# A state-space scan feeding a gated MLP: a new order of the first group's scan, weight conversion in wider pieces and in place, and state products side by side

## The chip, the cores and the metric

The kernel runs on one NeuronCore of a Trainium2 chip. Its engines work side by side, each through its own queue in order: TensorE (PE) multiplies matrices, VectorE (DVE) and ScalarE (ACT) work on elements, GpSimd (POOL) does small work, and SyncE (SP) issues most DMA transfers. An instruction whose input is not there holds everything behind it on its engine. The metric is device time in microseconds (us). Before the change the median of three runs is 408.18 us (408.10 to 408.22).

## The reference, cut to what matters

The first part is a Mamba-2 style scan over 4 batches of 8 heads, 768 positions, head size 32, state size 16. With `a` the decays, it is computed in chunks:

```
for c in chunks:
    cum = cumsum(log(clip(a, 1e-6, 1)))           # within the chunk
    L   = exp(cum_i - cum_j) for i >= j, else 0
    y   = ((C @ B.T) * L) @ x + (C @ state) * exp(cum)
    state = exp(sum(log a)) * state + sum_j B_j x_j * exp(cum_last - cum_j)
```

The second part takes the heads side by side as 3072 tokens of 256 features:

```
h = x @ w_in                       # 256 -> 2048
g = h * sigmoid(1.702 * h)
out = g @ w_out                    # 2048 -> 256
```

The weights arrive as 64-bit floats and the kernel makes 32-bit floats of them.

## The kernel before, in words

**Groups and pairs.** The 3072 tokens are six groups of 512 (`NG`). A group is two *pairs* (`p`) of 128-position chunks (`k` = 0, 1). Each group goes through a scan, then the MLP: sixteen `hidden` steps h0 to h15 (line 551: two matmuls each, then a SiLU into gT on ScalarE, line 554), and a projection. Group 0 projects with `project_all`: sixteen steps f0 to f15 of four matmuls (line 570) that add up in the two PSUM banks o0 and o1. Groups 1 to 5 interleave hidden steps with seven-product blocks (`product`, line 616).

**The scan of a pair.** The steps are functions. `pick_a` spreads decays by ScalarE; `fan` (line 310) broadcasts them by matmul; `decay_heads` (line 333) or, for later pairs, `decay` (line 292) runs VectorE scans that give L; `ends` (line 350) multiplies B by L's last column (Be). `turn_only` transposes B and C (line 418) and copies them out by ScalarE (BT, CT, C); `since_start` (line 439) scales C by the decay since the chunk's batch began, which `fan_rows` and `decay_fanned` or `decay_rows` make. `score` (line 454) computes C B^T in the PSUM area cb, `weigh` (line 465) multiplies L by it, `gain` (line 480) and `keep` (lines 494, 501) make the state, and `finish` adds up y: line 520 multiplies by states (`inter`), line 529 by L, and ScalarE copies y into yT (line 537). In `finish`, `inter` for k = 0 comes first, then the 16 products with L, then `inter` for k = 1 where the pair is not first of its batch.

**The weights.** They are cut in 16 pieces, eight of w_in and eight of w_out, of two 128-wide tiles each. `fetch` loads a piece (bits, 512 KB); eight bits buffers allow six loads ahead. `unpack` makes from the low words m (ScalarE, line 147), and from the high words e (VectorE, line 148: the exponent), z and p2 (ScalarE, lines 152, 153: a power of two) and u (VectorE, line 154: the mantissa). `join` then makes three VectorE passes: m += u - 7 (168), sign into p2 (170), and their product into w_in or w_out (176). The buffers e and z are single; u, m and p2 are double. `narrow(i)` unpacks piece i + 1 and then joins piece i.

**Order.** The program is written in the order in which every engine is to execute it, and `in_order` pins each engine to that order at the end. The scan of group 0 (pairs 0 and 1) is written out by hand ahead of the first hidden step. In hidden and project of group 0 the tables `in_hidden[0]` and `in_project[0]` say after or before which step a narrow, a scan step of pairs 2 and 3, or a load is placed. PSUM banks of the tag ff are four and go around between h, y, o, transposes and small products, so a new tile waits for the reader of the one whose bank it takes. The DMA queue of SP takes its transfers in order too.

Of the kernel before, what the change touches and what calls it, by code (L numbers as in the profile page):

```python
# [8 lines left out]
FP32 = mybir.dt.float32  # L9
U32 = mybir.dt.uint32  # L10
# [24 lines left out]
def kernel(  # L35
# [77 lines left out]

    PF = 2
    AHEAD = 6
    assert 2 * CG * PF == NF
    PIECES = [("in", f) for f in range(0, NF, PF)] + [("out", f) for f in range(0, NF, PF)]
    PN = PF * DM
    bits = {}

    def fetch(i, queue=nc.sync):
        if i >= len(PIECES):
            return
        name, f = PIECES[i]
        bits[i] = t = wide.tile([P, 2 * PN], U32, tag="bits", name=f"bits{i}", bufs=AHEAD + 2)
        if name == "in":
            src = moe_w_in[:, 2 * f * P:2 * (f + PF) * P].rearrange("(k p) e -> p k e", p=P)
            dst = t.rearrange("p (k e) -> p k e", k=NK)
        else:
            src = moe_w_out[f * P:(f + PF) * P, :].rearrange("(f p) e -> p f e", p=P)  # L130
            dst = t.rearrange("p (f e) -> p f e", f=PF)
        queue.dma_start(out=dst, in_=src)

    parts = {}

    def unpack(i):


        fetch(i + AHEAD)
        words = bits.pop(i).rearrange("p (e w) -> p e w", w=2)  # L140
        lo, hi = words[:, :, 0], words[:, :, 1]
        e = wide.tile([P, PN], U32, tag="e", name=f"e{i}", bufs=1)
        u = wide.tile([P, PN], U32, tag="u", name=f"u{i}")
        m = wide.tile([P, PN], FP32, tag="m", name=f"m{i}")
        z = wide.tile([P, PN], FP32, tag="z", name=f"z{i}", bufs=1)
        p2 = wide.tile([P, PN], U32, tag="p2", name=f"p2{i}")
        nc.scalar.activation(m, lo, AF.Copy, scale=2.0 ** -52)  # L147
        nc.vector.tensor_scalar(out=e, in0=hi, scalar1=0x7FF00000, scalar2=None,
                                op0=ALU.bitwise_and)


        nc.scalar.activation(z, e, AF.Relu, scale=-8.0, bias=edge[:, 0:1])  # L152
        nc.scalar.activation(p2, z, AF.Relu, scale=-1.0, bias=edge[:, 1:2])
        nc.vector.tensor_scalar(out=u, in0=hi, scalar1=0x000FFFFF, scalar2=0x41000000,
                                op0=ALU.bitwise_and, op1=ALU.bitwise_or)
        parts[i] = hi, u, m, p2

    def narrow(i):
        if i + 1 < len(PIECES):
            unpack(i + 1)  # L160
        join(i)

    def join(i):

        name, f = PIECES[i]
        hi, u, m, p2 = parts.pop(i)

        nc.vector.scalar_tensor_tensor(out=m, in0=u.bitcast(FP32), scalar=-7.0, in1=m,
                                       op0=ALU.add, op1=ALU.add)
        nc.vector.scalar_tensor_tensor(out=p2, in0=hi, scalar=0x80000000, in1=p2,  # L170
                                       op0=ALU.bitwise_and, op1=ALU.bitwise_or)
        if name == "in":
            dst, split = w_in[:, :, f * P:(f + PF) * P], NK
        else:
            dst, split = w_out[:, f:f + PF, :], PF
        nc.vector.tensor_tensor(  # L176
            out=dst, in0=m.rearrange("p (k e) -> p k e", k=split),
            in1=p2.bitcast(FP32).rearrange("p (k e) -> p k e", k=split), op=ALU.mult)


# [3 lines left out]
    def spread(n):  # L184
        if n - 4 in ra:
            ra[n] = ra[n - 4]
        else:
            ra[n] = wide.tile([P, NH * P], FP32, tag="bits", name=f"a{n}", bufs=AHEAD + 2)
        b, c = divmod(n, NC)
        nc.sync.dma_start(  # L190
            out=ra[n].rearrange("p (h i) -> p h i", h=NH),
            in_=scratch[b, c].unsqueeze(0).to_broadcast([P, NH, P]))
# [25 lines left out]
    rows_a(az, (nc.sync,))  # L218
    for i in range(2, AHEAD):
        fetch(i)  # L220
# [13 lines left out]
    for r in range(R):  # L234
# [3 lines left out]
                                channel_multiplier=1)  # L238


    whose = const.tile([32, NH, N], FP32, name="whose")
    nc.gpsimd.memset(whose, 1.0)
    nc.gpsimd.affine_select(out=whose, in_=whose, pattern=[[-1, NH], [0, N]],
                            compare_op=ALU.is_equal, fill=0.0, base=0, channel_multiplier=1)

    ident = const.tile([P, P], FP32, name="ident")
    make_identity(nc, ident)
    idents = const.tile([P, NH, P], FP32, name="idents")
    nc.gpsimd.tensor_copy(idents, ident.unsqueeze(1).to_broadcast([P, NH, P]))

# [11 lines left out]
    nc.gpsimd.tensor_tensor(out=own, in0=same[:, :HB], in1=same[:, HB:], op=ALU.add)  # L262

    starts = {}

    def clip(t, name):

        nc.vector.tensor_scalar(out=t, in0=t, scalar1=1e-6, scalar2=1.0,
                                op0=ALU.max, op1=ALU.min)
        starts[name] = const.tile([P, t.shape[1], 1], FP32, name=f"starts{name}")  # L270
        nc.vector.tensor_copy(starts[name], t[:, :, 0:1])
        nc.vector.memset(t[:, :, 0:1], 0.0)

    clip(az0, 0)


# [19 lines left out]

    fans, flat = {}, {}

    def pick_a(p):

        b, c = divmod(2 * p, NC)
        X = fans[p] = ssd.tile([P, 2, Q, P], FP32, tag="CT", name=f"X{p}")
        for q in range(Q):
            nc.scalar.activation(X[:, :, q], (az if c + 2 > CG else az0)[:, c:c + 2], AF.Copy,
                                 scale=pick[:, b, q:q + 1])

    def fan(p, r, ab):
# [5 lines left out]

    def fan_all(p):
        ab = area(f"ab{p}")
        for r in range(R):
            fan(p, r, ab[:, r])
        fans[p] = ab

# [7 lines left out]
    def decay_heads(p, r, ab):  # L327

        if r == 0:
# [6 lines left out]
            initial=0.0, op0=ALU.mult, op1=ALU.add)  # L336

    def decay_pair(p, engine=nc.vector):
        ab = fans.pop(p)
        for r in range(R):  # L340
            decay_heads(p, r, ab[:, r])
        ends(p, 0, engine)
        ends(p, 1, engine)

# [160 lines left out]

    def finish(p):
        g, half = divmod(p, PG)
# [16 lines left out]

        inter(0 if c else 1, True, False)
        for k in range(2):
            for h in range(NH):
                t, q = divmod(h, HB)
                nc.tensor.matmul(  # L529
                    out=y[t][D * q:D * q + D, k], lhsT=rx[p][:, k, h],  # L530
                    rhs=L[:, k, h // Q, h % Q],
                    start=False, stop=True, tile_position=(0, D * q), skip_group_check=True)
        if c:
            inter(1, False, True)
# [49 lines left out]
    def mix_w(n):  # L584

        t = wide.tile([P, 2, 4, P], FP32, tag="bits", name=f"mw{n}", bufs=AHEAD + 2)
        w = w_out[:, 4 * n:4 * n + 4].rearrange("p (j i) (c e) -> p j i c e", i=2, c=2)
# [73 lines left out]

    rows_zero()
    keep_busy(2)
    for p in range(PG):
        pick_a(p)
    for r in range(R):
        fan_one(0, r)
    for r in range(R):
        decay_heads(0, r, ab[0, r])
    ends(0, 0, nc.gpsimd)  # L670
    ends(0, 1, nc.gpsimd)
    fan_rows(0, CG)
    decay_fanned(0, CG)
    turn_only(0)
    score(0)
    unpack(0)
    fan_one(1, 0)
    fan_one(1, 1)
    weigh(0)
    decay_heads(1, 0, ab[1, 0])  # L680
    decay_heads(1, 1, ab[1, 1])
    gain(0)
    fan_one(1, 2)
    fan_one(1, 3)
    keep(0)
    since_start(0)
    decay_heads(1, 2, ab[1, 2])
    decay_heads(1, 3, ab[1, 3])
    fans.clear()
    turn_only(1)  # L690
    score(1)
    ends(1, 0, nc.gpsimd)
    ends(1, 1, nc.gpsimd)
    finish(0)
    since_start(1)
    gain(1)
    weigh(1, (0, 1))
    keep(1)
    finish(1)
    join(0)  # L700
    clip(az, 1)
    for b in range(NB):
        nc.sync.dma_start(out=scratch[b].rearrange("c h s -> h c s"),
                          in_=az[b * NH:(b + 1) * NH])
    unpack(1)
    narrow(1)

# [9 lines left out]
    in_project = [{} for _ in range(NG)]  # L717
    for i, k in zip(range(2, 10), (0, 1, 3, 5, 6, 8, 13, 14)):
        at(in_hidden[0], k, lambda i=i: narrow(i))
    at(in_hidden[0], 7, lambda: pick_a(PG))  # L720
    at(in_hidden[0], 8, lambda: fan_rows(CG, NC), lambda: decay_fanned(CG, NC))
    at(in_hidden[0], 9, lambda: fan_all(PG), lambda: decay_pair(PG))
    for k in range(2):
        at(in_hidden[0], 1 + 2 * k, lambda k=k: spread(CG + 2 + k))
        at(in_hidden[0], 15, lambda k=k: decay(CG + 2 + k))
    for i, k in zip(range(10, 16), (2, 3, 5, 7, 9, 11)):
        at(in_project[0], k, lambda i=i: narrow(i))
    scan_at(in_project[0], PG, (0, 1, 4, 6))
# [121 lines left out]
```

## Time and profile before

| What | us |
|---|---|
| Median of the runs | 408.18 |
| Time of the profiled execution | 408.12 |
| Its span | 406.4 |
| First h matmul | 33.99 |
| Hidden steps of group 0 end, first transpose of pair 2 | 65.1 |
| First h matmul of group 1 | 103.06 |
| TensorE busy | 387.3 |
| VectorE busy | 233.5 |
| ScalarE busy | 121.0 |

The profile is of one execution. A busy time is the time in which an instruction of that engine was running. A line of the order of time gives the start, the length, the engine, the line of the kernel, the operation, what it writes and reads, the count, and in brackets how long the engine stood idle before and which instruction's end released it. A matmul of 32-bit floats is two records. PEld is the loading of weights into the array. DMA shares are means over 16 DMA engines.

### The profile page before, as it was taken

How to read it: one execution, taken by the hardware profiler on the slowest of the kernel's cores; microseconds unless marked ns; L12 is line 12 of the kernel's file. 1: busy time of each engine (PE TensorE's matmuls, PEld its weight loads, DVE VectorE, ACT ScalarE, POOL GpSimd, SP SyncE). 2: the span in 40 equal slices, each digit the busy share in tenths (PEclk: the TensorE clock that was granted, in tenths of full speed). 3: DMA queues.
4: the chain of work that ended last, by engine and by line, in shares of the span. 5: the costliest groups of instructions: out<-in, count | busy, mean ns of one | idle time of the engine just before them, and what ended most of it. 6: DMA issues, size and time to landing. Idle time of an engine off the chain costs nothing.

```text
span 406.4 us, 5086 instructions
## 1 busy us (share of the span) xinstructions
PE 387.3 (95%) x2012; PEld 246.3 (61%) x2012; DVE 233.5 (57%) x380; ACT 121.0 (30%) x229; POOL 10.5 (3%) x32
## 2 busy tenths in 40 slices
PE   5787999899999999999999999999999999999984
PEld 1443446678556678566668566668566668466662
DVE  1888998994779877753574753563651311531312
ACT  3316967460332212231212231212322211312111
POOL 5000000010000001000000000000000000000000
PEclk9999999999999999999999999999999999999999
DMA  9988735930898200078000070000010000000001
GB/s 155 268 133 231 247 117 123 163 129 2 122 252 110 62 0 2 0 253 110 2 0 0 2 258 2 0 0 2 0 53 0 2 0 0 29 24 0 0 2 52
DMA packets 86126, 29.52 MB, mean 73 GB/s; under 512 B 75800, under 2 KB 79064, under 8 KB 86104
## 3 DMA queue, kind: packets, MB, share of 16 engines
q1 hardware_dynamic: 81848, 28.55, 29.9%
q10 hardware_dynamic: 4256, 0.66, 1.0%
q8 instruction: 16, 0.26, 0.3%
q14 instruction: 6, 0.05, 0.0%
HBM read 25.95 MB, written 3.24 MB: 72 GB/s over the span
## 4 chain that ended last, share of the span: by engine, by line
PE 81%; SPq 5%; DVE 4%; DMA 4%; ACT 3%; issue 2%; ACTq 0%; DVEq 0%
PE h L551 37%; PE acc L616 30%; SPq L111 5%; PE o L570 4%; PE y L529 3%; PE cb L454 2%; PE y L520 2%; DMA af<-in_a_dram 1%; DMA bits<-in_moe_w_in_dram 1%; ACT z L152 1%; DVE L L292 1%; PE oT L648 1%; PE tp L418 1%; DMA c<-in_C_dram 1%; ACT m L147 1%
## 5 line engine op out<-in xcount | busy, mean ns | idle before, releaser
L551 PE MATMUL h<-yT,w_in 128*128 128x512 f32 x384 | 173.1, 596 | 2.9 <-DVE w_in L176 2.4
L551 PEld LDWEIGHTS h<-yT,w_in 128*128 128x128 f32 x384 | 71.6, 190 | 80.5 <-issue 71.8
L554 ACT ACTIVATE gT<-h 128x512 f32<-128x512 f32 x96 | 56.9, 595 | 171.1 <-PE h L551 133.4
L600 DVE TENSOR_TENSOR mg<-gT 128x512 f32<-128x512 f32 x40 | 27.6, 689 | 95.6 <-ACT gT L554 92.4
L616 PE MATMUL acc<-mg,mw 128*128 128x256 f32 x240 | 58.3, 379 | 0.7 <-ACT u L629 0.7
L616 PEld LDWEIGHTS acc<-mg,mw 128*128 128x128 f32 x240 | 45.5, 190 | 7.3 <-ACT u L629 1.1
L616 PE MATMUL acc<-gT,w_out 128*128 128x256 f32 x160 | 41.7, 384 | 0.6 <-DVE u L640 0.6
L292 DVE TENSOR_TENSOR_SCAN L<-a,idents 128x1024 f32<-128x1024 f32 x18 | 41.1, 2283 | 0.0
L616 PEld LDWEIGHTS acc<-gT,w_out 128*128 128x128 f32 x160 | 29.5, 190 | 15.6 <-issue 11.5
L465 DVE TENSOR_TENSOR L<-L,cb 128x2048 f32<-128x2048 f32 (+1 forms) x13 | 27.5, 2122 | 9.3 <-PE cb L454 9.3
L570 PE MATMUL o<-w_out,gT 128*128 128x256 f32 x128 | 29.6, 384 | 0.8 <-DVE w_out L176 0.8
L570 PEld LDWEIGHTS o<-w_out,gT 128*128 128x128 f32 x128 | 23.7, 190 | 5.0 <-DVE w_out L176 1.2
L616 PE MATMUL acc<-gT,mw 128*128 128x256 f32 x80 | 23.6, 380 | 0.8 <-DVE c L640 0.8
L616 PE MATMUL acc<-mg,w_out 128*128 128x256 f32 x80 | 23.6, 380 | 0.8 <-DVE u L640 0.8
L454 PE MATMUL cb<-CT,BT 32*128 32x256 f32 x192 | 15.6, 445 | 2.4 <-ACT CT L425 2.4
L602 DVE TENSOR_TENSOR mg<-gT,mg 128x256 f32<-128x256 f32 x40 | 17.0, 425 | 1.4
L601 DVE TENSOR_TENSOR mg<-gT,mg 128x256 f32<-128x256 f32 x40 | 17.0, 425 | 1.4
L616 PEld LDWEIGHTS acc<-gT,mw 128*128 128x128 f32 x80 | 15.1, 190 | 3.3 <-DVE c L640 1.2
L616 PEld LDWEIGHTS acc<-mg,w_out 128*128 128x128 f32 x80 | 15.1, 190 | 3.2 <-DVE u L640 1.2
L640 DVE TENSOR_TENSOR u<-acc,u 128x256 f32<-128x256 f32 (+1 forms) x10 | 5.6, 559 | 19.8 <-ACT u L629 14.0
L537 ACT ACTIVATE yT<-y 128x256 f32<-128x256 f32 x24 | 8.0, 380 | 28.9 <-PE y L520 16.1
L333 DVE TENSOR_TENSOR_SCAN L<-ab,idents 128x512 f32<-128x512 f32 x12 | 13.8, 1205 | 4.5 <-PE ab L310 4.5
(82 smaller groups left out, 275.2 us busy)
## 6 DMA issues: line engine op xcount, KB each, us to landing
a<-scratch SPq DMA_DIRECT2D x18, 512.0 KB, 7.0
bits<-in_moe_w_in_dram SPq DMA_DIRECT2D x8, 512.0 KB, 5.9
bits<-in_moe_w_out_dram SPq DMA_DIRECT2D x8, 512.0 KB, 4.3
out_dram<-ob SPq DMA_DIRECT2D x12, 256.0 KB, 2.2
x<-in_x_dram SPq DMA_DIRECT2D x20, 128.0 KB, 3.5
b<-in_B_dram SPq DMA_DIRECT2D x24, 64.0 KB, 3.2
c<-in_C_dram SPq DMA_DIRECT2D x24, 64.0 KB, 4.9
af<-in_a_dram SPq DMA_DIRECT2D x3, 384.0 KB
```

The costliest lines, as they stand in the source:

```text
L111: queue.dma_start(out=dst[p][:, k], in_=src[b, :, sl, :].rearrange("h s d -> s h d"))
L292: nc.vector.tensor_tensor_scan(out=Ls[p][:, k].rearrange("p r q i -> p (r q i)"), data0=ra[n], data1=idents.rearrange("p h i -> p (h i)"), ...
L333: nc.vector.tensor_tensor_scan(out=flat[p][:, r], data0=ab, data1=idents.rearrange("p h i -> p (h i)")[:, :2 * Q * P], initial=0.0, op0=AL ...
L454: nc.tensor.matmul(out=cb[:, r, k], lhsT=BT[rows, k], rhs=CT[rows, k].rearrange("p q i -> p (q i)"), start=True, stop=True, tile_position= ...
L465: nc.vector.tensor_tensor(out=Lv[:, k], in0=Lv[:, k], in1=cb.rearrange("p r k e -> p k r e")[:, k], op=ALU.mult)
L551: nc.tensor.matmul(out=h, lhsT=w_in[:, k, f * P:(f + 1) * P], rhs=yT[g][:, k], start=(k == 0), stop=(k == NK - 1))
L554: nc.scalar.activation(gT[g, j][:, i], h, AF.Silu, scale=GELU_SCALE)
L570: nc.tensor.matmul(out=o[k // 2][:, k % 2], lhsT=gT[g, f // 2][:, f % 2, k * P:(k + 1) * P], rhs=w_out[:, f], start=(f == 0 and k % 2 == 0 ...
L600: nc.vector.tensor_tensor(out=t[:, 0:2], in0=B[:, :, 1], in1=B[:, 0], op=ALU.subtract)
L601: nc.vector.tensor_tensor(out=t[:, 2], in0=B[:, 1, 1], in1=t[:, 0], op=ALU.subtract)
L602: nc.vector.tensor_tensor(out=t[:, 3], in0=B[:, 1, 0], in1=t[:, 2], op=ALU.subtract)
L616: nc.tensor.matmul(out=acc[g][:, i], lhsT=lhsT, rhs=rhs, start=(j == 0 and i % 2 == 0), stop=(j == NF // 2 - 1), skip_group_check=True)
```

## The change

It has three parts.

1. **The first group's scan.** The hand-written order of pairs 0 and 1 changes on all engines: fans and scans are interleaved, the transposes of pair 0 come ahead of the since-start row and those of pair 1 directly after the weighting of pair 0, since_start of pair 1 comes before its weighting, and part of the conversion of pieces 0 and 1 is moved. There are three warming matmuls instead of two. `clip`, `pick_a` and the identity tiles are made earlier. The tile X takes a buffer of the output tile ob. Clipping the whole of `a` and storing it to the scratch tensor (`store_a`) moves from ahead of h0 to after h4.
2. **The weights.** There are ten pieces: four of two tiles (in 0 to 7), then six of four tiles. Bits buffers are four of twice the size, and also hold two spread rows of `a` or two sets of mixed weights. `fetch` is called at named places only. u is written over the low words, e, z and p2 share a tile, and m is a step of its own, `lower`. `narrow(i)` now joins piece i, then fetches, then lowers piece i + 2, then unpacks piece i + 1.
3. **State products of y.** In `finish` the `inter` of k = 1 stands directly after that of k = 0, except for pair 1.

Lines of the diff that matter, with parts left out:

```diff
-    PF = 2
-    AHEAD = 6
-    PIECES = [("in", f) for f in range(0, NF, PF)] + [("out", f) for f in range(0, NF, PF)]
+    PIECES = [("in", f, 2) for f in range(0, 8, 2)] + [("in", 8, 4), ("in", 12, 4)] \
+        + [("out", f, 4) for f in range(0, NF, 4)]
+    PN = 4 * DM
+    BUFS = 4
+    def words(name):
+        return wide.tile([P, 2 * PN], U32, tag="bits", name=name, bufs=BUFS)
...
+    def lower(i):
+        low[i] = wide.tile([P, PN], FP32, tag="m", name=f"m{i}")[:, :PIECES[i][2] * DM]
+        nc.scalar.activation(low[i], bits[i][0], AF.Copy, scale=2.0 ** -52)
     def unpack(i):
-        fetch(i + AHEAD)
...
-        nc.scalar.activation(m, lo, AF.Copy, scale=2.0 ** -52)
+        e = wide.tile([P, PN], U32, tag="p2", name=f"p2{i}")[:, :PIECES[i][2] * DM]
         nc.vector.tensor_scalar(out=e, in0=hi, scalar1=0x7FF00000, scalar2=None,
                                 op0=ALU.bitwise_and)
+        z = e.bitcast(FP32)
         nc.scalar.activation(z, e, AF.Relu, scale=-8.0, bias=edge[:, 0:1])
-        nc.scalar.activation(p2, z, AF.Relu, scale=-1.0, bias=edge[:, 1:2])
-        nc.vector.tensor_scalar(out=u, in0=hi, scalar1=0x000FFFFF, scalar2=0x41000000,
+        nc.scalar.activation(e, z, AF.Relu, scale=-1.0, bias=edge[:, 1:2])
+        power[i] = e
+        nc.vector.tensor_scalar(out=lo, in0=hi, scalar1=0x000FFFFF, scalar2=0x41000000,
                                 op0=ALU.bitwise_and, op1=ALU.bitwise_or)
-    def narrow(i):
-        if i + 1 < len(PIECES):
-            unpack(i + 1)
-        join(i)
+    NEXT = {4: (7,), 5: (8,), 7: (9,)}
+    def narrow(i):
+        join(i)
+        for n in NEXT.get(i, ()):
+            fetch(n)
+        if i + 2 < len(PIECES):
+            lower(i + 2)
+        if i + 1 < len(PIECES):
+            unpack(i + 1)
...
+        if c and not late:
+            inter(1, False, False)
         for k in range(2):
             for h in range(NH):
...
-        if c:
+        if c and late:
             inter(1, False, True)
...
-    rows_zero()
-    keep_busy(2)
-    for p in range(PG):
-        pick_a(p)
+    keep_busy(3)
     for r in range(R):
         fan_one(0, r)
-    for r in range(R):
         decay_heads(0, r, ab[0, r])
+    rows_zero()
+    lower(0)
+    turn_only(0)
+    fan_rows(0, CG)
+    decay_fanned(0, CG)
     ends(0, 0, nc.gpsimd)
     ends(0, 1, nc.gpsimd)
-    fan_rows(0, CG)
-    decay_fanned(0, CG)
-    turn_only(0)
+    unpack(0)
     score(0)
-    unpack(0)
-    fan_one(1, 0)
-    fan_one(1, 1)
     weigh(0)
-    decay_heads(1, 0, ab[1, 0])
-    decay_heads(1, 1, ab[1, 1])
+    turn_only(1)
+    for r in range(2):
+        fan_one(1, r)
+        decay_heads(1, r, ab[1, r])
     gain(0)
-    fan_one(1, 2)
-    fan_one(1, 3)
     keep(0)
     since_start(0)
-    decay_heads(1, 2, ab[1, 2])
-    decay_heads(1, 3, ab[1, 3])
-    fans.clear()
-    turn_only(1)
-    score(1)
+    for r in range(2, R):
+        fan_one(1, r)
+        decay_heads(1, r, ab[1, r])
     ends(1, 0, nc.gpsimd)
     ends(1, 1, nc.gpsimd)
-    finish(0)
     since_start(1)
-    gain(1)
+    lower(1)
+    score(1)
     weigh(1, (0, 1))
+    finish(0)
+    gain(1)
     keep(1)
-    finish(1)
-    join(0)
-    clip(az, 1)
-    for b in range(NB):
-        nc.sync.dma_start(out=scratch[b].rearrange("c h s -> h c s"),
-                          in_=az[b * NH:(b + 1) * NH])
-    unpack(1)
-    narrow(1)
+    finish(1, late=True)
+    narrow(0)
+    join(1)
+    fetch(6)
+    lower(3)
...
-    for i, k in zip(range(2, 10), (0, 1, 3, 5, 6, 8, 13, 14)):
+    at(in_hidden[0], 0, lambda: unpack(2))
+    for i, k in ((2, 1), (3, 3), (4, 6), (5, 9), (6, 13)):
         at(in_hidden[0], k, lambda i=i: narrow(i))
+    at(in_hidden[0], 4, store_a)
     at(in_hidden[0], 7, lambda: pick_a(PG))
     at(in_hidden[0], 8, lambda: fan_rows(CG, NC), lambda: decay_fanned(CG, NC))
-    at(in_hidden[0], 9, lambda: fan_all(PG), lambda: decay_pair(PG))
+    at(in_hidden[0], 10, lambda: fan_all(PG))
+    for i, k in ((7, 1), (8, 5), (9, 9)):
+        at(in_project[0], k, lambda i=i: narrow(i))
     for k in range(2):
-        at(in_hidden[0], 1 + 2 * k, lambda k=k: spread(CG + 2 + k))
-        at(in_hidden[0], 15, lambda k=k: decay(CG + 2 + k))
-    for i, k in zip(range(10, 16), (2, 3, 5, 7, 9, 11)):
-        at(in_project[0], k, lambda i=i: narrow(i))
+        at(in_hidden[0], 5 + k, lambda k=k: spread(CG + 2 + k))
+        at(in_project[0], 3 + 3 * k, lambda k=k: decay(CG + 2 + k))
```

## The prediction

> **What bounds the kernel now.** I read the page first (busy times, then the chain that ended last), then busy time by stage, then the order of time from 0 to 105 us.
>
> ```profile
> PE 387.3 (95%) x2012; PEld 246.3 (61%) x2012; DVE 233.5 (57%) x380; ACT 121.0 (30%) x229; POOL 10.5 (3%) x32
> ...
> PE 81%; SPq 5%; DVE 4%; DMA 4%; ACT 3%; issue 2%; ACTq 0%; DVEq 0%
> ```
>
> TensorE is 81% of the chain, so only what fills its idle time or takes work off it can help. By stage (columns: PE, PEld, DVE, ACT, POOL busy):
>
> ```profile
> 0.00:34.00 34.00, 24.77 (x173) 12.57 (x173) 21.68 (x36) 9.84 (x22) 7.21 (x23) 1.00 0.94 182
> 34.00:65.10 31.10, 29.64 (x76) 12.78 (x77) 28.72 (x56) 25.00 (x43) 0.74 (x1) 1.00 0.60 194
> 65.10:103.10 38.00, 36.50 (x271) 29.37 (x270) 31.09 (x48) 16.22 (x30) 1.24 (x3) 1.00 0.46 98
> ```
>
> The three rows are the start (before the first h matmul), hidden 0 and project 0. Hidden and project hold only 1.46 and 1.50 us of TensorE idleness, so the change can save little there and lose much. The start is a relay between engines. The order of time shows its last legs:
>
> ```profile
> 9.95 4.57 DVE L333 TENSOR_TENSOR_SCAN L<-ab,idents 128x512 f32<-128x512 f32 x4 [4.20 <-PE ab L310]
> 18.02 2.29 DVE L465 TENSOR_TENSOR L<-L,cb 128x2048 f32<-128x2048 f32 x1 [1.54 <-PE cb L454]
> 28.04 2.35 DVE L465 TENSOR_TENSOR L<-L,cb 128x1024 f32<-128x1024 f32 x2 [1.50 <-PE cb L454]
> 33.16 0.69 DVE L176 TENSOR_TENSOR w_in<-m,p 128x512 f32<-128x512 f32 x1
> 33.99 3.67 PE L551 MATMUL h<-yT,w_in 128*128 128x512 f32 x8 [1.43 <-DVE w_in L176]
> ```
>
> VectorE stands 1.5 us before each weighting, for the scores. Then the weight conversion, whose overlap decides the rest:
>
> ```profile
> 41.89 0.71 ACT L152 ACTIVATE z<-e,edge 128x512 f32<-128x512 uint32 x1
> 42.33 0.68 DVE L170 SCALAR_TENSOR_TENSOR p<-bits,p 128x512 uint32<-128x512 uint32 x1
> 42.62 0.72 ACT L153 ACTIVATE p<-z,edge 128x512 uint32<-128x512 f32 x1
> 43.04 0.69 DVE L176 TENSOR_TENSOR w_in<-m,p 128x512 f32<-128x512 f32 x1
> 43.65 0.42 DVE L148 TENSOR_SCALAR e<-bits 128x512 uint32<-128x512 uint32 x1
> ```
>
> ScalarE makes z and p2 of the next piece while VectorE joins this one. The period is 2.6 us (43.04 to 45.64) for two h tiles, which take TensorE 3.44 (4 records of 0.43 each). VectorE stays ahead.
>
> [...] 512-column records are 0.86 us apart at the start, 0.43 later. [...] 8 fan records take 1.07 us warm, not 3.4. [...] No 1024-wide conversion is in the trace. [...]
>
> **The change, part by part.** The changed program's order on each engine (no times in it) says who waits for whom; I put the measured durations on it. Joining piece i here means its L168, L170, L176.
>
> *Start.* VectorE's list is now nearly gapless: scans 9.95 to 14.55, carry and since 1.3, e and u 0.75, weighting 0 from 16.45 to 18.7 (before 20.3); the second pair's fan arrives 19.1; two scans 2.3; keep and since_start 0.95, to 22.4; two scans to 24.65; since_start 0.45; wait for Be on POOL to 25.3; weighting 1 to 27.65; keep 1.05; join(0) 2.0. w_in's first piece is ready at 30.75, before at 33.85: **gain 3.1**. The third warming matmul makes the first busy stretch 5.1 us long instead of 3.8. [...] If so fans and scores run at full clock and the piece is ready at 29.4: gain 4.5. I take the mean, 3.8.
>
> *Conversion.* narrow(i) now joins i first and unpacks i+1 after it. Nothing of i+1 can overlap the join: e waits (in VectorE's order) for the product, z for e, p2 for z, the next join for p2. And m of piece i+2 takes the buffer of piece i, so it waits for that product, at the head of ScalarE's queue, with z, p2 and the gT copies behind it. Period of a narrow piece: e 0.34 past the product + 0.09 + m's push and a gT 0.7 + z, p2 1.47 + sign 0.7 + product 0.7 = 4.0, against 3.44. Of a wide one: m 1.1, z 1.17, p2 1.17, sign 1.26, product 1.22 = 5.95, against 6.88 for four h. Cold start, product ends: join(0) 30.75, (1) 34.3, (2) 38.4, (3) 42.3, (4) 48.3. h2 waits 0.1, h4 0.6, h6 0.6; h8 waits for the first wide piece with only h6 and h7 to cover it: 5.95 - 3.44 = **2.5 us stall**. So h0 starts at 30.9, h2 34.5, h4 38.5, h6 42.5, h8 48.4. Before, hidden lost 1.46 in all. Width itself saves: a wide piece costs VectorE 4.7 us (0.6 + 0.6 + 1.13 + 1.13 + 1.22) against 5.2 for two narrow ones, but VectorE would now wait for ScalarE, so the saving goes into that wait.
>
> Next: rows and starts (0.9, after h8) hold VectorE to 51.3, since 0.8, join(5) 52.1 to 55.7, mask and u 1.2: scans of pair 2 start 56.9. They are 4.57 + Be 0.58 + join(6) 3.6: first w_out at 65.6. Then e of piece 7, and on ScalarE m, z, p2 (1.0 + 1.17 + 1.05), and only then gT of h14, at 69.5. The second bank of o waits for that gT (its bank). From scans to there: 12.7 us; TensorE has 5 h, a transpose and half of f0, 9.9, and reaches the wait early by the difference and the 0.9 that VectorE started late: **stall about 3.7**. Before, o started at 65.95 with none.
>
> Project: CsT of pair 2 waits for CT behind gT h15: 71.2. From it VectorE and ScalarE are serial to yT: 0.35 + join(7) 3.53 + 1.2 + state 0.6 + scan and Be 2.54 + weighting 2.2 + join(8) 3.53 + e 0.8 + z9, p9 2.2 + yT 0.4 = 17.4, 88.6. z9 and p9 stand before yT on ScalarE and wait for join(8); today the unpack ahead of this yT also follows the weighting, but its e (80.06) comes before the join, and yT runs at 81.96. The transposes of pair 3 need yT's bank: 88.6, before 83.5. TensorE has some 14.2 to do meanwhile from 69.6: **stall about 4 to 5** with its wait for the weighting. From there TensorE is the bound as before (19.5 to 103.06). So group 1 starts **5.1 later cold, 3.7 later warm; mean +4.4**.
>
> *y products.* Four k=1 records move beside the k=0 ones. Today:
>
> ```profile
> 80.19 1.08 PE L529 MATMUL y<-L,x 128*32 128x128 f32 x32 [0.66 <-DVE L L465]
> 81.20 0.49 PE L520 MATMUL y<-CsT,S 64*128 64x128 f32 x4
> ```
>
> A block of four costs 0.43, of which 0.2 is the switch. Saving 0.43 at most, 0 at least; I take 0.21 for each of the six such pairs after group 0: **-1.3** (0 to -2.6).
>
> *At nothing.* Two 1 MB fetches instead of 512 KB put 1 MB ahead of pair 2's loads on SP. At 10 to 20 us DMA moved 0.26 MB/us, so about 4 us later; those loads are used after 61. Piece 6 is issued past af (about 36), lands about 43, used 48.4: 5 us of cover, beyond which it delays piece 5 too. clip of az and its stores move into hidden 4: 0.85 us of VectorE, inside its wait for p2 (44.3 against 45.8); the spreads are used at 77. X in ob's buffers, paired a and mw tiles, ends inside fan_all, idents earlier on POOL (it waits anyway): same instructions, no TensorE wait.
>
> *Sum.* Span 406.4 + 4.4 - 1.3 = 409.5; the profiled execution's own time is 1.7 over its span (408.12), the median 408.18: **411.2**. In-place u with strided output: same 0.42 assumed[...].
>
> **Rivals.** *R1, faster:* the place is narrow in hidden and project 0. Hidden is held by VectorE's occupancy, not by the length of one piece's relay; the six wide pieces (0.5 us each) then free it, TensorE loses no more than today, and what the start gained reaches the end: 408.2 - 3.8 - 1.3 = 403.1; half of it, 405.6. It decides once the stalls together lose less than 5.1 us (3.8 + 1.3) more than today. For: VectorE was 92% busy in hidden (28.7 of 31.1). Against: the order, in which every step of a piece waits for the step before it on the other engine. *The change without its effect:* if the wait for scores just moves behind the fans, the start gains 1 instead of 3.8: 414, inside R3's numbers. *R2, no change:* losses and gains cancel, 407.4 to 409. *R3, worse:* SP becomes the bound: piece 6 or 7 lands after use, 413 to 416. For: DMA share 0.94 in the start. Against: 5 us of cover.
>
> **How the numbers follow.** Likeliest 0.64 (409.3 to 413.5 alone: start +-0.7, wide durations 5%, y +-0.6), R3 0.06, R2 0.08, R1 0.22. Range 406.0 to 414.8 leaves the lower half of R1 and the top of R3 out. 0.2% (0.8 us) is about what the measurement can tell from no change: faster 0.22, same 0.08, slower 0.70.
>
> **What would show it.** First h matmul at 29.5 to 31 (33.99 now); VectorE idle before the sign step with ScalarE's p2 as releaser; TensorE idle before h8 on w_in, before o on gT with m of ScalarE late, before pair 3's transposes on yT; L520 in blocks of eight, about 0.63. Wrong if TensorE's idle time in hidden and project together stays below 6 us, or if the start does not shorten.

## The result, and the profile after

After the change the median is 411.75 us (four runs, 410.76 to 412.73), before it 408.14 beside it on the same chip. The ratio is 1.0090, with a 95% interval of 1.0060 to 1.0119: slower by some 3.6 us. The forecast was 411.2. The profiled execution of the changed kernel took 410.76 us, the lowest of the four, its span 409.0. A second profile, of 412.46 us (span 410.8), is used further below.

The page after, its busy times and its chain that ended last:

```profile
PE 387.2 (95%) x2014; PEld 246.5 (60%) x2014; DVE 230.4 (56%) x350; ACT 117.4 (29%) x211; POOL 12.1 (3%) x32
...
PE 80%; DVE 11%; ACT 5%; issue 1%; DMA 1%; SPq 0%; POOL 0%; ACTq 0%; DVEq 0%
```

TensorE has the same busy time as before (387.2, before 387.3), and VectorE and ScalarE have 3 to 4 us less each. But VectorE's share of the chain went from 4% to 11%, and ScalarE's from 3% to 5%. Less work, more waiting for it. Busy time in the second and third of the windows shown of before (PE, PEld, DVE, ACT, POOL, then the granted clock):

```profile
34.00:65.10 31.10, 28.73 (x78) 12.54 (x76) 26.08 (x35) 22.46 (x31) 0.74 (x1) 1.00 0.56 166
65.10:103.10 38.00, 33.67 (x242) 26.31 (x243) 26.61 (x28) 11.79 (x19) 2.92 (x3) 0.91 0.45 103
```

TensorE is idle for 2.4 and 4.3 us in them, where it was idle for 1.5 and 1.5. The start in order of time:

```profile
23.59 2.35 DVE L478 TENSOR_TENSOR L<-L,cb 128x1024 f32<-128x1024 f32 x2 [0.30 <-POOL Be L363]
28.22 0.69 DVE L178 TENSOR_TENSOR w_in<-m,p 128x512 f32<-128x512 f32 x1
```

VectorE no longer waits for scores: both waits of 1.5 us are gone, and the last one left is 0.30 for Be. The weightings start at 15.22 and 23.59 (before 18.02 and 28.04), and the first piece of w_in is ready at 28.91 instead of 33.85: **4.9 us gained**. The conversion, VectorE and ScalarE in order of time, with the first wide piece (its end is the wait of h8):

```profile
39.82 0.69 DVE L178 TENSOR_TENSOR w_in<-m,p 128x512 f32<-128x512 f32 x1
...
40.55 1.22 ACT L148 ACTIVATE m<-bits 128x1024 f32<-128x1024 uint32 x1 [0.51 <-DVE w_in L178]
...
42.82 1.15 ACT L159 ACTIVATE p<-p,edge 128x1024 uint32<-128x1024 f32 x1
44.00 1.23 DVE L172 SCALAR_TENSOR_TENSOR p<-bits,p 128x1024 uint32<-128x1024 uint32 x1 [0.34 <-ACT p L159]
45.26 1.22 DVE L178 TENSOR_TENSOR w_in<-m,p 128x1024 f32<-128x1024 f32 x1
```

From one product (L178) to the next everything follows in single file: m, z, p2, sign, product. From the end of the narrow piece's product at 40.51 to that of the wide one at 46.48 it takes 5.97. TensorE pays for it here:

```profile
46.63 1.96 PE L566 MATMUL h<-yT,w_in 128*128 128x512 f32 x4 [1.69 <-DVE w_in L178]
...
67.48 2.07 PE L585 MATMUL o<-w_out,gT 128*128 128x256 f32 x4 [2.73 <-ACT gT L569]
...
87.53 0.44 PE L431 MATMUL tp<-ident,b 128*128 128x128 f32 x2 [1.95 <-ACT yT L552]
...
107.03 3.60 PE L566 MATMUL h<-yT,w_in 128*128 128x512 f32 x8
```

h8 waits for w_in, the second bank of o for a gT, the transposes of pair 3 for yT. Group 1 starts at 107.03, where it started at 102.90. (The 103.06 in the table of the times before is from the view of the chain, which lets a piece begin only where the one before it ends; in that view it is 107.19 now. The starts here and below are from the order of time.) Behind the second and third wait stands ScalarE's queue:

```profile
63.54 1.19 ACT L148 ACTIVATE m<-bits 128x1024 f32<-128x1024 uint32 x1 [3.20 <-DVE w_out L178]
...
66.85 1.06 ACT L569 ACTIVATE gT<-h 128x512 f32<-128x512 f32 x2
...
84.88 1.15 ACT L158 ACTIVATE p<-p,edge 128x1024 f32<-128x1024 uint32 x1 [8.53 <-DVE p L153]
...
87.11 0.64 ACT L552 ACTIVATE yT<-y 128x256 f32<-128x256 f32 x2
```

y was complete at 83.66 (its products with L, L544, start at 82.58 and take 1.08). Its copy runs 3.45 us later, because z and p2 of a piece stand ahead of it on ScalarE and wait for VectorE.

So the balance of the span, 409.0 - 406.4 = +2.6: start -4.9, from the first h of group 0 to the first h of group 1 **+9.1** (77.97 instead of 68.91), the rest -1.5 (301.97 instead of 303.50). The +9.1 is not waiting alone: TensorE is idle for 6.7 us of that stretch instead of 3.0, and busy for 71.3 instead of 65.9 with the same products. Most of the second part is half clock: the granted clock was 0.50 up to 32.9 and again from 67.1 to 73.9.

### The profile page after: what moved, and what is told of

Its sections match the earlier page's. It is cut to its first block, busy times and chain, and to the rows that moved or that the text cites. A ratio compares the mean times of both kernels' runs of the same rounds, so it can differ in the third digit from the quotient of the medians.

```text
span 409.0 us, 5001 instructions
## 1 busy us (share of the span) xinstructions
PE 387.2 (95%) x2014; PEld 246.5 (60%) x2014; DVE 230.4 (56%) x350; ACT 117.4 (29%) x211; POOL 12.1 (3%) x32
## 4 chain that ended last, share of the span: by engine, by line
PE 80%; DVE 11%; ACT 5%; issue 1%; DMA 1%; SPq 0%; POOL 0%; ACTq 0%; DVEq 0%
PE h L566 35%; PE acc L634 30%; PE o L585 6%; DVE L L353 3%; PE cb L467 3%; PE y L544 2%; DVE p L172 2%; DVE L L478 2%; ACT p L159 1%; PE y L533 1%; DVE w_in L178 1%; ACT p L158 1%; ACT m L148 1%; PE tp L431 1%; PE oT L666 1%
## 5 line engine op out<-in xcount | busy, mean ns | idle before, releaser
L566 PE MATMUL h<-yT,w_in 128*128 128x512 f32 x384 | 175.0, 601 | 3.2 <-DVE w_in L178 3.0
L634 PEld LDWEIGHTS acc<-gT,w_out 128*128 128x128 f32 x160 | 29.5, 190 | 15.9 <-issue 11.5
L585 PE MATMUL o<-w_out,gT 128*128 128x256 f32 x128 | 32.8, 412 | 2.8 <-ACT gT L569 2.7
L585 PEld LDWEIGHTS o<-w_out,gT 128*128 128x128 f32 x128 | 25.5, 205 | 8.3 <-ACT gT L569 3.1
```

The lines of the kernel that those rows point to most:

```text
L566: nc.tensor.matmul(out=h, lhsT=w_in[:, k, f * P:(f + 1) * P], rhs=yT[g][:, k], start=(k == 0), stop=(k == NK - 1))
L585: nc.tensor.matmul(out=o[k // 2][:, k % 2], lhsT=gT[g, f // 2][:, f % 2, k * P:(k + 1) * P], rhs=w_out[:, f], start=(f == 0 and k % 2 == 0 ...
L634: nc.tensor.matmul(out=acc[g][:, i], lhsT=lhsT, rhs=rhs, start=(j == 0 and i % 2 == 0), stop=(j == NF // 2 - 1), skip_group_check=True)
```

## The experiments

Below, "stretch" is the time from the first h matmul of group 0 to the first of group 1 in the kernel's profiled execution: the conversion has its place in it, and neither the start nor the later groups do. Each ratio is to the kernel before on the same chip.

### The parts alone

The theory: the start and the y products gain what the prediction said, and the conversion loses more than both. The rival R1: the conversion loses less than 5.1 us.

Only the new y, on the kernel before:

```diff
         inter(0 if c else 1, True, False)
+        if c and not late:
+            inter(1, False, False)
...
-        if c:
+        if c and late:
             inter(1, False, True)
```

> The kernel before with only the state products of y side by side. Forecast's step: 0.2 us saved at each of the seven pairs that get it, 406.8 (group 1's start to the end 1.3 shorter). Rival, no switch is saved: 408.1. Upper end: 405.2.

Measured: 406.45 us, ratio 0.9961 (0.9948 to 0.9973).

Only the new start (the hand-written order, three warming matmuls, and X in a buffer of ob; not the earlier `clip` and `pick_a`, nor the move of `store_a`), with pieces and conversion of before:

> The kernel before, its 512 KB pieces and its conversion kept, with only the new order of pairs 0 and 1 and three warming matmuls. If the start's gain is real and the conversion of before passes it on: first h matmul at 29 to 30.5, time 403.5 to 405. Rival, VectorE's occupancy in hidden swallows it: first h as early, but 407 to 408.

Measured: 404.51 us, ratio 0.9910 (0.9892 to 0.9928); first h at 30.59.

Both together:

> The kernel before with the new start and the y products, without the wider pieces: the two gains add to 402 to 403.5 if they are independent. If the change's loss lies in the start or in y, it stays above 408.

Measured: **403.11 us**, ratio 0.9876 (0.9859 to 0.9894). The same kernel in another set of runs:

> The kernel with the new start and the new y and the old conversion, once more beside the three edits: 402.5 to 404 us.

Measured: 403.38 us, ratio 0.9886 (0.9868 to 0.9904). The two gains of 1.7 and 3.7 nearly add up, to 4.7 to 5.1. This version beats both kernels. What is left of the change, the conversion with the small moves around it, costs 411.75 - 403.1 = 8.6 us (R1 had it below 5.1). Its VectorE work in this better version, in order of time (the profile of the second set, whose first h starts at 30.24):

```profile
34.09 0.69 DVE L176 TENSOR_TENSOR w_in<-m,p 128x512 f32<-128x512 f32 x1
...
39.29 0.69 DVE L176 TENSOR_TENSOR w_in<-m,p 128x512 f32<-128x512 f32 x1
...
51.50 4.56 DVE L334 TENSOR_TENSOR_SCAN L<-ab,idents 128x512 f32<-128x512 f32 x4 [0.32 <-PE ab L311]
```

The two products shown are two pieces apart, so the period is 2.60 us. A piece is used by two h steps, which take TensorE 3.44. The scans of pair 2 can start at 51.5.

### What of the conversion costs: order, place or width

Three edits to the 403.1 us kernel, all with the narrow pieces. First, only the order of join and unpack:

```diff
     def narrow(i):
+        join(i)
         if i + 1 < len(PIECES):
             unpack(i + 1)
-        join(i)
```

> The kernel with the new start and the new y (narrow pieces, 403.1 us), and in narrow(i) the join of piece i ahead of the unpack of piece i + 1, as the changed kernel has it; pieces stay two tiles wide, u, e and z keep their own tiles. My theory, that the order makes a relay: the period of a narrow piece is e after the product 0.43, z and p2 on ScalarE 1.45 with a SiLU of 0.6 in between for half of the pieces, sign 0.70, product 0.69, so 3.3 to 3.9 us against 3.44 of TensorE's work; the period of 4.0 of the changed kernel is reached only with m at the head of ScalarE's queue, which is free here. TensorE waits for w_in in most hidden steps, VectorE for p2 about 1 us in each of some 14 pieces, and scans and w_out are late: 405.5 to 409. The rival, that only the pieces' width or the writing in place costs: 402.5 to 404.5, with no wait of VectorE for p2.

Measured: **412.22 us**, ratio 1.0101 (1.0085 to 1.0118). The order alone costs 8.8 to 9.1 us, all of what the whole new conversion costs, and more than either expectation had. VectorE, ScalarE and TensorE in order of time:

```profile
39.27 0.69 DVE L170 SCALAR_TENSOR_TENSOR p<-bits,p 128x512 uint32<-128x512 uint32 x1 [0.47 <-ACT p L153]
...
51.19 0.72 ACT L152 ACTIVATE z<-e,edge 128x512 f32<-128x512 uint32 x1 [0.84 <-DVE e L148]
...
52.57 0.58 ACT L557 ACTIVATE gT<-h 128x512 f32<-128x512 f32 x1
53.20 3.78 PE L554 MATMUL h<-yT,w_in 128*128 128x512 f32 x4 [2.97 <-ACT gT L557]
58.84 4.57 DVE L334 TENSOR_TENSOR_SCAN L<-ab,idents 128x512 f32<-128x512 f32 x4 [3.26 <-PE ab L311]
```

The period is 3.36 us (products start at 39.99 and 43.35), still below the 3.44 of two h steps, and VectorE idles only 0.47 per piece. The loss comes by another way than I had expected. The table does not place one narrow every two steps: narrows 2 to 6 stand behind h0, h1, h3, h5 and h6, and ScalarE, which works in order, has their passes between the gT of h0 and that of h7. These two gT are five periods apart, 16.8 us (35.78 to 52.57), where TensorE's seven steps take 12.0 at full clock. With the unpack first they are 13.1 apart (34.65 to 47.74). So z waits on ScalarE for e (0.84), the gT waits behind z and p2, its PSUM bank comes free late, and TensorE waits 2.97 us for that bank, where it waited 0.46. The four h records behind it then take 3.78 us instead of 1.98, at a granted clock of 0.50 (window 52 to 57). The fan of pair 2 comes behind them, and its scans start at 58.84, 7.3 us later than without the edit.

Second, only the writing in place:

```diff
-        e = wide.tile([P, PN], U32, tag="e", name=f"e{i}", bufs=1)
-        u = wide.tile([P, PN], U32, tag="u", name=f"u{i}")
+        u = lo
...
-        z = wide.tile([P, PN], FP32, tag="z", name=f"z{i}", bufs=1)
-        p2 = wide.tile([P, PN], U32, tag="p2", name=f"p2{i}")
+        p2 = e = wide.tile([P, PN], U32, tag="p2", name=f"p2{i}")
+        z = e.bitcast(FP32)
```

> The kernel with the new start and the new y (403.1 us), narrow pieces and the unpack first, and only the writing in place from the changed kernel: u over the low words, e, z and p2 in one tile. u then waits on VectorE for m of the same piece, and m of a piece needs the product two pieces before: m can begin with that product and takes 0.72, e meanwhile 0.42, so u is late by at most 0.4 us for a piece whose VectorE work is 2.6 of 3.44 us; and e no longer waits for the single e buffer. My theory, that writing in place alone costs little: 402.5 to 405. The rival, that it takes away the slack that the two engines need to overlap: 406 or more, with VectorE waits for m ahead of u.

Measured: 409.33 us (nine runs, 407.19 to 411.12), ratio 1.0033 (1.0013 to 1.0054), 6 us above the kernel without it. My theory fell, the rival stands. In order of time:

```profile
38.51 0.43 DVE L153 TENSOR_SCALAR bits<-bits 128x512 uint32<-128x512 uint32 x1 [0.29 <-ACT m L146]
...
49.70 3.45 PE L553 MATMUL h<-yT,w_in 128*128 128x512 f32 x4 [1.91 <-ACT gT L556]
...
61.50 0.60 ACT L556 ACTIVATE gT<-h 128x512 f32<-128x512 f32 x1 [1.12 <-PE h L553]
61.99 0.66 ACT L146 ACTIVATE m<-bits 128x512 f32<-128x512 uint32 x1
62.68 0.43 DVE L153 TENSOR_SCALAR bits<-bits 128x512 uint32<-128x512 uint32 x1 [2.70 <-ACT m L146]
...
76.78 5.41 PE L572 MATMUL o<-w_out,gT 128*128 128x256 f32 x16 [2.34 <-DVE w_out L175]
```

u of piece i + 1 overwrites the words that m of piece i + 1 is made from, so it waits for that m, and the join of piece i is behind it on VectorE. In its own tile u needed no m: m of i + 1 had time until the next join. The wait is only 0.29 per piece, but m now waits for the product in turn, and the period is 3.11 instead of 2.60. The gT of h7 is five periods behind that of h0 here too (33.54 to 49.08, 15.5 us): at 49.70 TensorE waits 1.91 us for its bank, and the four records behind it take 3.45 instead of 1.98, at half clock. The fan of pair 2 starts 23.9 us after the first h, 20.05 without the edit: half of the loss is there already (0.9 of it from h0 and h1, at half clock left over from the start). At 61.99 m stands behind a SiLU whose matmul is only just done, VectorE loses 2.70, its conversion of w_out falls behind, and at f8 TensorE waits 2.34 us for w_out; the sixteen records after that take 5.41 instead of 3.72, at half clock.

Third, both:

> Both of these edits together on the kernel with the new start and the new y (403.1 us): joined first and in place, pieces still two tiles wide. This is all of the changed kernel's conversion but its width, its lowering two pieces ahead and its places. If the order is the cause and in place is not, the same as joined first alone within 1 us; if the two only cost together, 2 us or more above the sum of their single costs. If width is the cause of most of the 8.5 us, both together stay below 406; if not, 407 to 411.

Measured: 412.75 us, ratio 1.0103 (1.0072 to 1.0133): within 1 us of joined first alone, and above the range that was given. The costs don't add up: 9 for the order, 6 for the place, 9.5 for both, as I read it because, joined first, nothing is left to overlap. And these narrow pieces cost what the changed kernel's wide ones do (411.75, and 412.88 below). **The width, with the lowering two pieces ahead and the new places that come with it, costs nothing that can be told here; the order does, and in-place writing does where the order is mended.**

That is also what the changed kernel shows with its wide pieces kept, unpacked first from piece 2 on:

```diff
     def narrow(i):
+        if i > 1 and i + 1 < len(PIECES):
+            unpack(i + 1)
         join(i)
...
-        if i + 1 < len(PIECES):
+        if i <= 1:
             unpack(i + 1)
```

> The changed kernel with one edit: from piece 2 on, narrow unpacks piece i+1 ahead of joining piece i again. If the serial relay is the cause: the wait before h8 goes from 1.7 to near 0, the one before pair 3's transposes goes (yT some 3.5 us earlier), group 1 starts 4 to 6 us earlier, time 405.5 to 408. If the width itself, or the half clock, is the cause: 410.5 to 412.

The changed kernel once more, on the chip of the runs of the next two sections:

> The changed kernel once more, for the three runs beside it: 410.7 to 412.8, its two levels 1.7 us apart.

Measured: 409.2 us, ratio 1.0036 (1.0021 to 1.0051), against 412.88, ratio 1.0124 (1.0095 to 1.0154). It recovers 2.5 to 3.7 of the 4 to 6 expected, between the two ranges that were given, and lands where in-place alone lands (409.33). From its order of time:

```profile
38.68 0.70 DVE L162 TENSOR_SCALAR bits<-bits 128x1024 uint32<-128x1024 uint32 x1 [0.75 <-ACT m L148]
47.32 1.96 PE L568 MATMUL h<-yT,w_in 128*128 128x512 f32 x4 [1.62 <-DVE w_in L178]
...
66.18 1.10 PE L587 MATMUL o<-w_out,gT 128*128 128x256 f32 x4 [2.24 <-DVE w_out L178]
```

yT is copied at 82.56, 4.5 us earlier, and the wait of pair 3's transposes is gone. What is left is in the lines: u still waits 0.75 for m, h8 1.62 for its piece, and the first o waits 2.24 for w_out, whose join now stands behind the next unpack. Half clock follows that wait too (after another of 0.46 the next four records take 2.00). Wide pieces with u in its own tile weren't tried, so in wide pieces the place is not timed apart.

The stretch in all these kernels, with TensorE's busy and idle time in it:

| Conversion, with new start and new y | us | Stretch, us | TensorE busy | idle |
|---|---|---|---|---|
| before, with old start and old y | 408.1 | 68.91 | 65.9 | 3.0 |
| as before (two profiles) | 403.1, 403.4 | 68.56, 68.54 | 65.8, 65.8 | 2.8, 2.7 |
| in place | 409.3 | 75.84 | 70.8 | 5.0 |
| in place, wide, unpack first | 409.2 | 74.76 | 69.8 | 5.0 |
| join first | 412.2 | 78.83 | 71.1 | 7.8 |
| join first, in place | 412.75 | 78.31 | 69.4 | 9.0 |
| join first, in place, wide (the change; two profiles) | 411.75, 412.9 | 77.97, 78.35 | 71.3, 68.6 | 6.7, 9.8 |

The products are the same in every row. So of the 9.4 to 9.8 us that the conversion adds to the stretch, 3.9 and 7.0 are waiting in the two profiles of the change, and 5.5 and 2.8 are slower work, mostly at half clock: behind the waits, and in the first profile also in the first hidden steps, where it is left over from the start. No run has the waits without the half clock, so how much of the cost would stay at full clock is not shown.

### One wait removed

In the changed kernel, the narrow of piece 6, whose m, z and p2 stand ahead of gT at f0, moved two steps later:

```diff
-    for i, k in ((2, 1), (3, 3), (4, 6), (5, 9), (6, 13)):
+    for i, k in ((2, 1), (3, 3), (4, 6), (5, 9), (6, 15)):
```

> The changed kernel with narrow(6) placed after h15 instead of h13, so that gT of h14 and h15 are ahead of m, z and p2 on ScalarE. The wait of o for gT (2.7 us) goes to below 0.5. If that wait sets the end: 408.5 to 409. If, as the forecast's chain has it, the serial stretch from CT of pair 2 to yT sets it: CT comes only about 1 us earlier, and with the half clock after the wait gone 2 us in all: 409.5 to 411.

Measured: 412.07 us, ratio 1.0120 (1.0097 to 1.0142), above both ranges that were given: no gain that can be told beside 412.88. The wait of 2.73 before o is gone, and TensorE's order of time has other ones in its place:

```profile
80.61 1.35 PE L544 MATMUL y<-L,x 128*32 128x128 f32 x32 [2.03 <-DVE L L478]
...
87.39 0.44 PE L431 MATMUL tp<-ident,b 128*128 128x128 f32 x2 [2.13 <-ACT yT L552]
```

Pair 3's transposes run 56.6 us after the first h (30.82), in the two profiles of the changed kernel 58.5 and 57.2. By the same count CT comes 0.6 us earlier than in the second of them, and so do the transposes: the chain from CsT to yT is as long (16.9), and VectorE and ScalarE, not TensorE's wait before o, set its end. The 0.6 is too little to tell in the time, and half clock follows both new waits (eight records of o take 3.37 and 3.38 where 1.99 and 1.89 would do).

### The clock

In the profile of the changed kernel the granted clock is 0.50 behind the wait before o. Three filler matmuls there (extra work, its result not used), and separately two warming matmuls instead of three at the start:

> The changed kernel with three more warming matmuls (their result is not used) where the second bank of o waits for gT. If the half clock after that wait holds the scores of pair 2 back (VectorE waited 1.2 us for them): group 1 starts about 1 us earlier, about 410.7 and less spread. If the slack before pair 3's transposes covers it: no change, 411.7.

> The changed kernel with two warming matmuls as before. The third is worth a full-clock first fan if it works: first w_in piece at about 30.4 to 30.8 instead of 28.9, time 1.2 to 1.9 longer, about 413.3. If the clock in the start doesn't matter: 411.7.

Measured: 411.92 us, ratio 1.0103 (1.0079 to 1.0126), and 412.93, ratio 1.0141 (1.0086 to 1.0196). Neither can be told from the changed kernel by its time. Both profiled executions had half clock at yet another place (0.76 and 0.74 over 50 to 63). The filler did keep full clock behind it (the next four records of o took 1.13), but then the transposes waited 3.70. With two warming matmuls the first fan took 2.09 and the first piece was ready at 31.21. Over all the kernels, the fan took 1.79 to 2.09 in the three profiles with two warming matmuls, and 1.14 in eight of the eleven with three (1.62 to 2.09 in the rest).

What half clock cost in the changed kernel is seen in its second profile, which ran at full clock through the wait before o (TensorE, order of time):

```profile
47.94 1.95 PE L566 MATMUL h<-yT,w_in 128*128 128x512 f32 x4 [2.30 <-DVE w_in L178]
...
68.78 1.13 PE L585 MATMUL o<-w_out,gT 128*128 128x256 f32 x4 [2.73 <-ACT gT L569]
...
87.54 0.44 PE L431 MATMUL tp<-ident,b 128*128 128x128 f32 x2 [3.70 <-ACT yT L552]
...
88.17 3.44 PE L585 MATMUL o<-w_out,gT 128*128 128x256 f32 x8
```

The transposes come at 87.54, in the first profile at 87.53, but the way there differs. The second starts h0 1.31 us later. The first loses as much behind o, where the scores of pair 2 come late at half clock and VectorE waits for them:

```profile
78.42 2.29 DVE L478 TENSOR_TENSOR L<-L,cb 128x2048 f32<-128x2048 f32 x1 [1.20 <-PE cb L467]
```

In the second that weighting starts at 78.44 with no wait. Then the wait of 3.70 is followed by half clock: the eight records at 88.17 take 3.44, in the first profile 1.89. With the slower transposes beside them that is the 1.7 us by which group 1 starts later in the second (108.72 and 107.03), and by which its time is longer.

## Why the prediction was right, point by point

- **Start.** Predicted ready at 30.75 with a cold fan, 29.4 with a warm one. I gave the two equal weight, an estimate that no trace showed. Measured 28.91 and 30.22 in the two profiles (first h at 29.06 and 30.37). The fan's eight records took 1.14 us in both (warm, against 2.09 before). In the second the clock fell just behind the fan, at 9.4, and transposes, scores and the second fan ran at half: the granted clock over the first 24 us was 0.70, in the first profile 0.93. That is neither of the two cases, and that it came near the cold one is luck. The gain was 4.9 and 3.6, the mean taken 3.8.
- **Conversion.** The relay was right in its steps and its lengths: periods of 4.03 and 5.97 between product ends (predicted 4.0 and 5.95), 17.57 from the first to the fifth (17.55). In the first profile ScalarE's 1024-wide z and p2 took 1.14 to 1.15, m 1.18 to 1.22; VectorE's mask took 0.68 to 0.69, sign and product 1.22 to 1.23. The lengths of the wide passes in the prediction were estimates of mine: the trace of before has no conversion that wide to show them. The order as the cause was right too: in narrow pieces, joining first alone costs as much.
- **Stall before h8.** Predicted 2.5, measured 2.30 in the second profile and 1.69 in the first. There the first hidden steps ran at half clock (granted 0.51 from 29 to 33), and so the small waits that I put before h2, h4 and h6 were filled with slower work.
- **Stall before o.** Predicted 3.7, measured 2.73 twice. From the scans (54.88) to o (67.48) it took 12.6, as worked out (12.7). But TensorE left the fan at 54.28, 0.6 ahead of the scans and not 0.9, and its work from there to the wait took 10.5 and not 9.9.
- **Stall before pair 3's transposes.** Predicted 4 to 5, measured 3.70 in the second profile, and 1.95 in the first, where TensorE was slowed to half clock ahead of it. The transposes came at 87.5 in both, predicted 88.6 from a cold start. The chain from CsT to yT measured 16.9, and 18.2 with a wait of 1.2 for cb in it, against 17.4.
- **Group 1.** Starts 4.1 us later in the first profile and 5.8 in the second; predicted were 3.7 warm and 5.1 cold. That these pair up is luck: the two starts had met again at pair 3's transposes, and the 1.7 between them is half clock behind the wait there.
- **The sum.** Here luck helped. The waits worked out between h0 and group 1 add up to 11.5 to 12.5 us (1.3, 2.5, 3.7, 4 to 5); measured was an idle time of 6.7 and 9.8. What made up for it is a term that the prediction had at nothing: half clock in hidden and project. TensorE was busy there for 5.5 and 2.8 us longer than in the kernel with the new start and y alone, mostly for that reason. So the sum came to 411.2 against 411.75 with waits too long and work too short.
- **y.** A block of eight takes 0.65 to the next matmul (82.58 - 81.93), against 0.63 assumed; a block of four takes 0.42 in the same profile (99.00 - 98.58), so setting two side by side saves some 0.2. The later groups took 1.5 less, predicted 1.3; alone on the kernel before it is 1.7 in all.
- **At nothing.** Right for the moves of loads and of store_a: no wait of TensorE or VectorE in the profile is for piece 6 or 7, and R3 did not happen. Not seen as a cost of its own: writing u in place. I had priced its strided output (same 0.42 assumed, 0.42 to 0.44 measured) but not its wait for m. In the changed kernel the order hides that; with the unpack first, in narrow pieces, it costs 6 us.
- **R1** was wrong for the reason given against it: VectorE's busy share fell (28.7 to 26.1 in the hidden window), and its waits on ScalarE took what it freed.
- TensorE's idle time in hidden and project was 6.7 us in the first profile, above the 6 that was set, but by little; in the second it was 9.8.

## What to carry to other kernels

Where two engines hand a piece back and forth, write the next piece's first half ahead of this piece's second half, and see what each buffer saved by writing in place makes wait: order and place cost 9 and 6 us here, and the change lost time though VectorE and ScalarE had less to do. Hold the period of a piece against the steps that really lie between two pieces, not against the steps that use one: 3.36 was below the 3.44 of two steps, but five pieces stood within seven steps that take 12.0 us together, or 2.4 each, and the PSUM readers queued behind them came late. When a change bundles several edits, time them apart: here two of the three gain 5 us, and the third loses 9.

## What the runs showed of the hardware

In the first profile of the change the granted clock was 0.50 from 67.06 to 73.88, behind the wait before o, and 1.00 on both sides of it, from 63 on and up to 78. But half clock did not follow every wait of TensorE, and the length of a wait does not tell it apart:

| Wait, run | us | Records behind it | us | at full clock |
|---|---|---|---|---|
| before o, the change, first profile | 2.73 | four of o | 2.07 | 1.13 |
| before o, the change, second profile | 2.73 | four of o | 1.13 | 1.13 |
| before h8, the change, second profile | 2.30 | four of h | 1.95 | 1.95 |
| before h8, the narrow of piece 6 later | 2.30 | four of h | 1.96 | 1.95 |
| before h8, three filler matmuls | 2.30 | four of h | 2.80 | 1.95 |
| before f8, in place | 2.34 | sixteen of o | 5.41 | 3.72 |
| before pair 3's transposes, the change, first profile | 1.95 | eight of o | 1.89 | 1.89 |
| the same, the change, second profile | 3.70 | eight of o | 3.44 | 1.89 |

What decides, these figures do not tell. So one and the same wait can cost something or nothing, and one profile alone doesn't show which.
